# The MLP behind a windowed attention rebuilt: wide units, one activation table, VectorE in GpSimd's place

## The chip, the cores and the metric

One core of one Trainium2 chip runs the whole program. The metric is the device time of one execution in microseconds (us), the median of several. The profile is one execution, recorded by the hardware's own profiler. Engine names: PE is TensorE (PEld its weight loads), ACT is ScalarE, DVE is VectorE, POOL is GpSimd, SP is SyncE, which here only issues DMAs.

## The reference, cut to what matters

Attention over 4 batches x 8 heads x 768 positions x 64 channels, where each position sees the 128 last positions and the first 4 ("sinks"). Its output, 3072 tokens x 512, goes through an MLP whose activation is a rational function of h:

```python
x = attn_out.transpose(0, 2, 1, 3).reshape(B * S, H * D)      # 3072 x 512
h = x @ w_in                                                  # 3072 x 2048
h2 = h * h
h3 = h2 * h
P = a[0] + a[1] * h + a[2] * h2 + a[3] * h3
Q = 1.0 + np.abs(b[0]) * np.abs(h) + np.abs(b[1]) * h2
g = P / (Q + 1e-06)
return (g @ w_out).astype(np.float32)                         # 3072 x 512
```

## The kernel before, in words

The program has two stages. **Attention** loops over the 32 heads. For each head three DMAs bring q, k and v (`q_in` and `v_in` on SP's queue, `k_in` on ACT's); they are cast to bf16, q and k are transposed on PE, and three pairs of 128-row tiles go through scores (`ps_s`), Exp on ACT (`e_t`), the mask product (`a_t`, on DVE for the first pair, on POOL for the other two), the product with v (`ps_o`), a reciprocal on DVE and a scaling (`o_bf`), and a transpose back (`ps_xall`). The last step of a head is the copy of `ps_xall` into the resident bf16 matrix `xT` (L199 before), so 32 of these copies mark the 32 heads. Four `xT` tiles of 128 rows hold the MLP's input, channels on the partitions.

**The MLP** loops over 6 blocks of 512 tokens, and in each over 8 chunks of 2 x 128 of the 2048 hidden channels, so 48 chunks of 128 partitions x 1024 elements. A chunk is eight matmuls into `ps_h` (two PSUM banks of fp32), then eleven elementwise operations on three engines: ACT takes Square and Abs straight from PSUM, DVE makes three linear forms of h*h (`t2`, `t1`, `sden`) and `u_num`, which reads PSUM, POOL adds `p_num` and `den`, ACT takes Ln and Exp(-x) of `den` as the reciprocal, and DVE multiplies to `g_t`:

```python
nc.gpsimd.tensor_tensor(out=p_num, in0=u_num, in1=t1, op=ALU.add)
nc.gpsimd.tensor_tensor(out=den, in0=sden, in1=hb, op=ALU.add)
nc.scalar.activation(out=lnq, in_=den, func=AF.Ln)
nc.scalar.activation(out=rden, in_=lnq, func=AF.Exp, scale=-1.0)
nc.vector.tensor_tensor(out=g_t, in0=p_num, in1=rden, op=ALU.mult)
```

After the eighth chunk of a block, four accumulations of 16 matmuls make `ps_out` (128 tokens x 512), ACT copies each to `o_t`, and SP's queue stores it.

The kernel's text gives no order between engines. A scheduler of the language orders each engine's instructions, and each engine runs its own list strictly in order; pools of `bufs` buffers decide when a tile may be written again. Pools that are closed give their memory to later ones, and the first writer of the later pool then waits for the last reader of the earlier.

At the start, POOL's queue (its DMAs cast fp32 to bf16 as they copy) issues the four loads of `w_in`, the sixteen of `w_out`, then `a_bc` and `b_bc` (the coefficients, broadcast to all partitions), while SP and ACT issue the first q, k, v.

Of the kernel before, what the change touches and what calls it, by code (L numbers as in the profile page):

```python
# [16 lines left out]
def kernel(  # L17
# [25 lines left out]
    const_pool = ctx.enter_context(tc.tile_pool(name="const", bufs=1))
    wpool = ctx.enter_context(tc.tile_pool(name="weights", bufs=1))
    xpool = ctx.enter_context(tc.tile_pool(name="xT", bufs=1))
# [16 lines left out]
        out=mask_prev, in_=ones_pp, pattern=[[-1, P]], compare_op=ALU.is_gt,  # L62
# [25 lines left out]
    a_bc = const_pool.tile([P, 4], FP32)  # L88
# [13 lines left out]
    with tc.tile_pool(name="a_in", bufs=2) as a_in, \  # L102
# [7 lines left out]
        for b in range(B):  # L110
            for h in range(H):
# [19 lines left out]
                for t in range(NT):  # L131
# [7 lines left out]
                                 start=True, stop=True)  # L139
# [64 lines left out]
    a0 = a_bc[:, 0:1]
    a1 = a_bc[:, 1:2]
    a2 = a_bc[:, 2:3]
    a3 = a_bc[:, 3:4]
    b0 = babs[:, 0:1]
    b1 = babs[:, 1:2]

    with tc.tile_pool(name="m_ps", bufs=2, space=bass.MemoryType.PSUM) as m_ps, \
         tc.tile_pool(name="m_sb", bufs=2) as m_sb, \
         tc.tile_pool(name="g_sb", bufs=2) as g_sb_pool, \
         tc.tile_pool(name="o_ps", bufs=2, space=bass.MemoryType.PSUM) as o_ps, \
         tc.tile_pool(name="o_sb", bufs=2) as o_sb:
        TW = 2 * TB
        for blk in range(NB):
            t0 = blk * TB
            g_chunks = []
            for fp in range(NFFC // 2):  # L220
                ps_h = m_ps.tile([P, 2, TB], FP32, tag="ps_h")
# [7 lines left out]
                s_sq = m_sb.tile([P, TW], BF16, tag="s_sq")
                nc.scalar.activation(out=s_sq, in_=ps_h, func=AF.Square)  # L230
                hb = m_sb.tile([P, TW], BF16, tag="hb")
                nc.scalar.activation(out=hb, in_=ps_h, func=AF.Abs, scale=b0)  # L232
                t2 = m_sb.tile([P, TW], BF16, tag="t2")
                nc.vector.tensor_scalar(out=t2, in0=s_sq, scalar1=a3, scalar2=a1,  # L234
                                        op0=ALU.mult, op1=ALU.add)
                t1 = m_sb.tile([P, TW], BF16, tag="t1")
                nc.vector.tensor_scalar(out=t1, in0=s_sq, scalar1=a2, scalar2=a0,  # L237
                                        op0=ALU.mult, op1=ALU.add)
                u_num = m_sb.tile([P, TW], BF16, tag="u_num")
                nc.vector.tensor_tensor(out=u_num, in0=ps_h, in1=t2, op=ALU.mult)  # L240
                p_num = m_sb.tile([P, TW], BF16, tag="p_num")
                nc.gpsimd.tensor_tensor(out=p_num, in0=u_num, in1=t1, op=ALU.add)  # L242
                sden = m_sb.tile([P, TW], BF16, tag="sden")
                nc.vector.tensor_scalar(out=sden, in0=s_sq, scalar1=b1, scalar2=1.000001,
                                        op0=ALU.mult, op1=ALU.add)
                den = m_sb.tile([P, TW], BF16, tag="den")
                nc.gpsimd.tensor_tensor(out=den, in0=sden, in1=hb, op=ALU.add)  # L247
                lnq = m_sb.tile([P, TW], FP32, tag="lnq")
                nc.scalar.activation(out=lnq, in_=den, func=AF.Ln)  # L249
                rden = m_sb.tile([P, TW], BF16, tag="rden")  # L250
                with nc.allow_low_precision(reason="exp(-ln(q)) reciprocal, tol 2e-2"):
                    nc.scalar.activation(out=rden, in_=lnq, func=AF.Exp, scale=-1.0)  # L252
                g_t = g_sb_pool.tile([P, TW], BF16, tag=f"g_{fp}")
                nc.vector.tensor_tensor(out=g_t, in0=p_num, in1=rden, op=ALU.mult)  # L254
                g_chunks.append(g_t)

            for tt in range(TB // P):
                ps_out = o_ps.tile([P, DM], FP32, tag="ps_out")
                for fc in range(NFFC):
                    fp, half = fc // 2, fc % 2  # L260
                    nc.tensor.matmul(ps_out,  # L261
                                     lhsT=g_chunks[fp][:, half * TB + tt * P:
                                                       half * TB + (tt + 1) * P],
                                     rhs=w_out_sb[fc],
                                     start=(fc == 0), stop=(fc == NFFC - 1))
                o_t = o_sb.tile([P, DM], FP32, tag="o_t")
                nc.scalar.activation(out=o_t, in_=ps_out, func=AF.Copy)
                row0 = t0 + tt * P
                nc.sync.dma_start(out=out[row0:row0 + P, :], in_=o_t)


# [33 lines left out]
```

## Time and profile before

| what | us |
|---|---|
| median of 3 runs (630.08 to 630.91) | 630.25 |
| span of the profiled execution, first to last instruction | 628.0 |
| so outside the span, by the median | 2.25 |
| start of the span to the first `xT` copy | 44.2 |
| first to last `xT` copy (31 heads) | 223.2 |
| last `xT` copy to the end of the last `g_t` | 346.2 |
| from there to the end of the span | 14.4 |

The stages are cut where an instruction that belongs to one of them ends it. The busy time of an engine in a stage, beside the stage's length, says whether it can be what sets the pace there; the durations of single instructions say what a changed one would cost.

### The profile page before, as it was taken

How to read it: one execution, taken by the hardware profiler on the slowest of the kernel's cores; microseconds unless marked ns; L12 is line 12 of the kernel's file. 1: busy time of each engine (PE TensorE's matmuls, PEld its weight loads, DVE VectorE, ACT ScalarE, POOL GpSimd, SP SyncE). 2: the span in 40 equal slices, each digit the busy share in tenths (PEclk: the TensorE clock that was granted, in tenths of full speed). 3: DMA queues.
4: the chain of work that ended last, by engine and by line, in shares of the span. 5: the costliest groups of instructions: out<-in, count | busy, mean ns of one | idle time of the engine just before them, and what ended most of it. 6: DMA issues, size and time to landing. Idle time of an engine off the chain costs nothing.

```text
span 628.0 us, 6817 instructions
## 1 busy us (share of the span) xinstructions
PE 448.3 (71%) x2208; PEld 209.6 (33%) x2208; DVE 353.8 (56%) x666; ACT 459.4 (73%) x602; POOL 309.9 (49%) x255
## 2 busy tenths in 40 slices
PE   2289998888888889946569566755846595567626
PEld 2145555555555555311123122211311231223102
DVE  1134444444444444397774976687397739766860
ACT  1265565555555555279999899999999999999891
POOL 4514433333334433256654664575467537645750
PEclk9999999999999999987779768977897787789667
DMA  9982233333333321000001000000100010000001
GB/s 191 203 162 53 63 76 82 84 75 77 77 77 86 78 64 39 1 0 1 1 0 67 2 0 34 34 0 1 50 18 0 0 67 1 0 33 35 0 0 67
DMA packets 81699, 29.80 MB, mean 47 GB/s; under 512 B 76032, under 2 KB 78080, under 8 KB 81664
## 3 DMA queue, kind: packets, MB, share of 16 engines
q1 hardware_dynamic: 53632, 18.88, 12.1%
q10 hardware_dynamic: 25088, 6.29, 4.5%
q0 software_dynamic: 2944, 4.20, 3.6%
q8 instruction: 17, 0.28, 0.2%
q14 instruction: 18, 0.15, 0.1%
HBM read 27.27 MB, written 6.29 MB: 53 GB/s over the span
## 4 chain that ended last, share of the span: by engine, by line
PE 30%; ACT 29%; DVE 16%; issue 14%; POOL 6%; DMA 5%; POOLq 0%; ACTq 0%; DVEq 0%
ACT L252 7%; ACT rden L252 6%; ACT lnq L249 5%; ACT L249 5%; PE ps_s L161 5%; PE ps_xall L196 5%; PE ps_tk L133 4%; DMA q_in<-in_q_dram 4%; DVE t L234 4%; PE ps_o L176 4%; PE ps_o L183 3%; POOL den L247 3%; PE ps_tq L132 3%; PE ps_sink L138 3%; DVE g_t L254 3%
## 5 line engine op out<-in xcount | busy, mean ns | idle before, releaser
L225 PE MATMUL ps_h<-xT,w_in_sb 128*128 128x512 bf16 x384 | 124.9, 474 | 65.1 <-DVE u_num L240 63.9
L247 POOL TENSOR_TENSOR den<-sden,hb 128x1024 bf16<-128x1024 bf16 x48 | 104.4, 2176 | 132.8 <-ACT hb L232 92.7
L261 PE MATMUL ps_out<-w_out_sb,g_t 128*128 128x512 bf16 x384 | 114.6, 452 | 65.9 <-DVE g_t L254 65.8
L171 POOL TENSOR_TENSOR a_t<-e_t,mask_pp 128x512 bf16<-128x512 bf16 x64 | 73.6, 1150 | 142.6 <-PE ps_o L179 117.3
L254 DVE TENSOR_TENSOR g_t<-p_num,rden 128x1024 bf16<-128x1024 bf16 x48 | 88.2, 1838 | 75.1 <-ACT rden L252 75.1
L242 POOL TENSOR_TENSOR p_num<-u_num,t 128x1024 bf16<-128x1024 bf16 x48 | 104.4, 2174 | 9.3 <-DVE u_num L240 9.3
L164 ACT ACTIVATE e_t<-ps_s 128x512 bf16<-128x512 f32 (+1 forms) x96 | 53.0, 554 | 54.0 <-POOL a_t L171 51.8
L225 PEld LDWEIGHTS <-w_in_sb 128*128 128x128 bf16 x384 | 43.9, 115 | 135.9 <-issue 108.5
L261 PEld LDWEIGHTS <-g_t 128*128 128x128 bf16 x384 | 39.1, 110 | 140.6 <-DVE g_t L254 91.0
L187 DVE RECIPROCAL recip<-ps_o 128x1 f32<-128x1 f32 x192 | 29.4, 164 | 99.6 <-PE ps_o L183 94.9
L190 ACT ACTIVATE o_bf<-ps_o,recip 128x64 bf16<-128x64 f32 x96 | 29.5, 307 | 54.6 <-DVE recip L187 52.0
L240 DVE TENSOR_TENSOR u_num<-ps_h,t 128x1024 bf16<-128x1024 f32 x48 | 58.6, 1220 | 16.8 <-ACT hb L232 16.8
L161 PE MATMUL ps_s<-qT,kT 64*128 64x128 bf16 x352 | 53.6, 301 | 13.8 <-ACT e_t L164 13.8
L249 ACT ACT_TABLE_LOAD x48 | 61.6, 1283 | 0.9
L252 ACT ACT_TABLE_LOAD x48 | 61.6, 1283 | 0.8
L249 ACT ACTIVATE lnq<-den 128x1024 f32<-128x1024 bf16 x48 | 50.8, 1058 | 15.2 <-POOL den L247 14.8
L232 ACT ACTIVATE hb<-ps_h,babs 128x1024 bf16<-128x1024 f32 x48 | 53.0, 1104 | 0.0
L252 ACT ACTIVATE rden<-lnq 128x1024 bf16<-128x1024 f32 x48 | 50.7, 1057 | 0.5
L230 ACT ACTIVATE s_sq<-ps_h 128x1024 bf16<-128x1024 f32 x48 | 48.5, 1011 | 1.7 <-PE ps_xall L196 1.7
L234 DVE TENSOR_SCALAR t<-s_sq,a_bc 128x1024 bf16<-128x1024 bf16 x48 | 47.5, 990 | 3.8 <-ACT s_sq L230 3.8
L196 PE MATMUL ps_xall<-ident,o_bf 128*64 128x128 bf16 x192 | 44.8, 311 | 3.0 <-ACT o_bf L190 2.0
L237 DVE TENSOR_SCALAR t<-s_sq,a_bc 128x1024 bf16<-128x1024 bf16 x48 | 45.6, 950 | 0.0
(51 smaller groups left out, 557.3 us busy)
## 6 DMA issues: line engine op xcount, KB each, us to landing
k_in<-in_k_dram ACTq DMA_DIRECT2D x32, 192.0 KB, 3.0
q_in<-in_q_dram SPq DMA_DIRECT2D x32, 192.0 KB, 2.7
v_in<-in_v_dram SPq DMA_DIRECT2D x32, 192.0 KB, 2.7
out_dram<-o_t SPq DMA_DIRECT2D x24, 256.0 KB, 2.0
w_in_sb<-in_moe_w_in_dram POOLq DMA_DIRECT2D x4, 512.0 KB, 10.9
w_out_sb<-in_moe_w_out_dram POOLq DMA_DIRECT2D x16, 128.0 KB, 7.5
a_bc<-in_moe_a_dram POOLq DMA_DIRECT2D x1, 2.0 KB, 6.4
b_bc<-in_moe_b_dram POOLq DMA_DIRECT2D x1, 1.0 KB, 5.8
```

What stands on the lines that cost most here:

```text
L161: nc.tensor.matmul(ps_s[:, co:co + P], lhsT=kT[:, kt * P:(kt + 1) * P], rhs=qT[:, t * P:(t + 1) * P], start=True, stop=True)
L171: nc.gpsimd.tensor_tensor(out=a_t[:, 0:ncols], in0=e_t[:, 0:ncols], in1=pmask, op=ALU.mult)
L196: nc.tensor.transpose(ps_xall[:, t * P:(t + 1) * P], o_bf, ident)
L225: nc.tensor.matmul(ps_h[:, half, :], lhsT=w_in_sb[c][:, fc * P:(fc + 1) * P], rhs=xT[c][:, t0:t0 + TB], start=(c == 0), stop=(c == NDMC - 1))
L234: nc.vector.tensor_scalar(out=t2, in0=s_sq, scalar1=a3, scalar2=a1, op0=ALU.mult, op1=ALU.add)
L240: nc.vector.tensor_tensor(out=u_num, in0=ps_h, in1=t2, op=ALU.mult)
L242: nc.gpsimd.tensor_tensor(out=p_num, in0=u_num, in1=t1, op=ALU.add)
L247: nc.gpsimd.tensor_tensor(out=den, in0=sden, in1=hb, op=ALU.add)
L249: nc.scalar.activation(out=lnq, in_=den, func=AF.Ln)
L252: nc.scalar.activation(out=rden, in_=lnq, func=AF.Exp, scale=-1.0)
L254: nc.vector.tensor_tensor(out=g_t, in0=p_num, in1=rden, op=ALU.mult)
L261: nc.tensor.matmul(ps_out, lhsT=g_chunks[fp][:, half * TB + tt * P: half * TB + (tt + 1) * P], rhs=w_out_sb[fc], start=(fc == 0), stop=(fc ...
```

## The change

The attention code is the same; the lists that the scheduler makes of it are not. The MLP's code is new:

- A unit is 4 x 128 hidden channels x 512 tokens, 128 x 2048 elements, so 24 units in place of 48 chunks.
- ACT copies `ps_h` from PSUM to a bf16 tile `hb` (two copies of 1024 for a unit), and all that follows reads `hb`.
- |h| is an AND of the pairs of bf16 numbers, taken as 32-bit words, with a mask that clears the two sign bits (`den`, 128 x 1024 words on DVE). h*h is a product on DVE, in every fourth unit a Square on ACT. The sum |h| + h*h, the odd and the even part of the numerator and their sum are DVE's; GpSimd has nothing left in the MLP.
- h is scaled by |b1|/|b0|, which is multiplied into `w_in` once. So `w_in` is no longer cast by its DMA: SP loads it as fp32 into two staging buffers (`t_f`, 1 MB each), and DVE scales and casts it. That needs `b_bc`, through `babs` (ACT) and a few tiny DVE operations to `csc`.
- Ln takes scale and bias as per-partition operands; one activation table, loaded at the start, holds all functions that are used.
- The units are pipelined by hand: unit i's projection, then Ln and Exp of unit i-1, then numerator and denominator of unit i, then one output tile of an earlier block, then `g_t` of unit i-1.

```diff
+    nc.scalar.preload_act_table_set("natural_log_exp_and_others")
...
-    w_in_sb = []
-    for c in range(NDMC):
-        t_in = wpool.tile([P, DF], BF16, name=f"w_in_sb_{c}")
-        nc.gpsimd.dma_start(out=t_in, in_=moe_w_in[c * P:(c + 1) * P, :])
-        w_in_sb.append(t_in)
...
+    csc = const_pool.tile([P, 1], FP32)
+    nc.vector.tensor_tensor(out=csc, in0=bpos[:, 1:2], in1=binv[:, 0:1], op=ALU.mult)
...
+    with tc.tile_pool(name="w_stage", bufs=2) as w_stage:
+        for c in range(NDMC):
+            t_f = w_stage.tile([P, DF], FP32, tag="w_in_f")
+            nc.sync.dma_start(out=t_f, in_=moe_w_in[c * P:(c + 1) * P, :])
+            t_in = wpool.tile([P, DF], BF16, name=f"w_in_sb_{c}")
+            nc.vector.tensor_scalar(out=t_in, in0=t_f, scalar1=csc, scalar2=None,
+                                    op0=ALU.mult)
+            w_in_sb.append(t_in)
...
+                nc.scalar.activation(out=hb[:, half * 2 * TB:(half + 1) * 2 * TB],
+                                     in_=ps_h, func=AF.Copy)
+            return hb
+
+        def numerator_and_denominator(i, hb):
+            s_sq = m_sb.tile([P, UW], BF16, tag="s_sq")
+            den = m_sb.tile([P, UW], BF16, tag="den")
+            if i % 4 == 3:
+                nc.scalar.activation(out=s_sq, in_=hb, func=AF.Square)
+            else:
+                nc.vector.tensor_tensor(out=s_sq, in0=hb, in1=hb, op=ALU.mult)
+            nc.vector.tensor_scalar(out=den.bitcast(U32), in0=hb.bitcast(U32),
+                                    scalar1=0x7FFF7FFF, scalar2=None,
+                                    op0=ALU.bitwise_and)
+            nc.vector.tensor_tensor(out=den, in0=den, in1=s_sq, op=ALU.add)
+            odd = m_sb.tile([P, UW], BF16, tag="odd")
+            nc.vector.tensor_scalar(out=odd, in0=s_sq, scalar1=a3, scalar2=a1,
+                                    op0=ALU.mult, op1=ALU.add)
+            num = m_sb.tile([P, UW], BF16, tag="num")
+            nc.vector.tensor_scalar(out=num, in0=s_sq, scalar1=a2, scalar2=a0,
+                                    op0=ALU.mult, op1=ALU.add)
+            nc.vector.tensor_tensor(out=odd, in0=odd, in1=hb, op=ALU.mult)
+            nc.vector.tensor_tensor(out=num, in0=num, in1=odd, op=ALU.add)
+            return den, num
+
+        def reciprocal(den):
+            lnq = m_sb.tile([P, UW], FP32, tag="lnq")
+            nc.scalar.activation(out=lnq, in_=den, func=AF.Ln, scale=qsc, bias=one_eps)
+            rden = m_sb.tile([P, UW], BF16, tag="rden")
+            with nc.allow_low_precision(reason="exp(-ln(q)) reciprocal, tol 2e-2"):
+                nc.scalar.activation(out=rden, in_=lnq, func=AF.Exp, scale=-1.0)
+            return rden
...
+        for i in range(len(units) + 1):
+            hb = project_in(i) if i < len(units) else None
+            rden = reciprocal(pend[1]) if pend is not None else None
+            nxt = None
+            if hb is not None:
+                den, num = numerator_and_denominator(i, hb)
+                nxt = (i, den, num)
+            if waiting:
+                project_out(*waiting.pop(0))
+            if pend is not None:
+                blk, u = units[pend[0]]
+                g_t = g_sb_pool.tile([P, UW], BF16, tag=f"g_{u}")
+                nc.vector.tensor_tensor(out=g_t, in0=pend[2], in1=rden, op=ALU.mult)
+                g_of[blk, u] = g_t
+                if u == NU - 1:
+                    waiting += [(blk, tt) for tt in range(ntt)]
+            pend = nxt
```

Two places of the built lists. The first is the head of ACT's list, at the start of the program. Before:

```order
L116 DMA k_in<-in_k_dram 128x6x64 x2
L121 ACT_TABLE_LOAD
L121 ACTIVATE q_bf<-q_in 128x384
L116 DMA k_in<-in_k_dram 128x6x64
L121 ACTIVATE q_bf<-q_in 128x384
```

The same place after the change (L143 is the load of k, L148 the cast of q, L90 the absolute value of the coefficients b):

```order
L44 ACT_TABLE_LOAD
L90 ACTIVATE babs<-b_bc 128x2
L143 DMA k_in<-in_k_dram 128x6x64 x2
L148 ACTIVATE q_bf<-q_in 128x384
L143 DMA k_in<-in_k_dram 128x6x64 x2
L161 ACTIVATE qT<-ps_tq 64x768
```

`babs`, which waits for the last DMA of POOL's queue, now stands ahead of the first load of k. In the same way SP's list now begins with the four loads of `t_f`, and the first q, k and v, whose buffers lie where the staging buffers were, wait for the fourth scaling of `w_in` on DVE.

The second place is DVE's list in the middle of the MLP. Before, one chunk (`t` is t2 and t1):

```order
L234 TENSOR_SCALAR t_4360<-s_sq,a_bc 128x1024
L237 TENSOR_SCALAR t_4362<-s_sq,a_bc 128x1024
L244 TENSOR_SCALAR sden<-s_sq,babs 128x1024
L240 TENSOR_TENSOR u_num<-ps_h,t_4360 128x1024
L254 TENSOR_TENSOR g_t<-p_num,rden 128x1024
```

After, one unit (`acoef` holds the rescaled coefficients a):

```order
L272 TENSOR_TENSOR s_sq<-hb 128x2048
L273 TENSOR_SCALAR den<-hb 128x1024
L278 TENSOR_SCALAR odd<-s_sq,acoef 128x2048
L276 TENSOR_TENSOR den<-den,s_sq 128x2048
L281 TENSOR_SCALAR num<-s_sq,acoef 128x2048
L283 TENSOR_TENSOR odd<-odd,hb 128x2048
L321 TENSOR_TENSOR g_t<-num,rden 128x2048
L284 TENSOR_TENSOR num<-num,odd 128x2048
```

Two chunks of five operations became one unit of eight, in every fourth unit seven (the first row is then ACT's). `g_t` in the seventh row belongs to the unit before, and stands behind three operations of the next unit that do not wait for ACT's Ln and Exp.

## Rows read from the trace of the kernel before

**Rows 1.** Busy time of each engine in four stages (clock granted, DMA share, GB/s behind).

```profile
core 0: us, PE busy (x) PEld busy (x) DVE busy (x) ACT busy (x) POOL busy (x), PEclk, DMA share, GB/s
0.00:44.20 44.20, 18.58 (x128) 12.33 (x128) 8.43 (x34) 15.51 (x31) 19.21 (x41) 1.00 1.04 193
44.20:267.40 223.20, 203.46 (x1331) 115.90 (x1331) 94.96 (x391) 114.29 (x261) 83.85 (x119) 1.00 0.29 66
267.40:613.60 346.20, 215.75 (x716) 77.31 (x716) 250.43 (x241) 327.20 (x308) 206.83 (x96) 0.80 0.04 16
613.60:628.00 14.40, 10.49 (x36) 4.04 (x36) 0.00 (x0) 2.39 (x4) 0.00 (x0) 0.82 0.20 73
```

**Rows 2.** Single lines on ACT in the MLP: ns min/median/max, first and last start.

```profile
L230 ACT ACTIVATE s_sq<-ps_h x48: 1002/1006/1034, 267.5 to 601.3; 128x1024 bf16<-128x1024 f32 x48
...
L232 ACT ACTIVATE hb<-ps_h,babs x48: 1092/1097/1135, 268.5 to 604.6; 128x1024 bf16<-128x1024 f32 x48
...
L252 ACT ACT_TABLE_LOAD  x48: 1283/1283/1283, 273.9 to 610.4; - x48
L252 ACT ACTIVATE rden<-lnq x48: 1056/1057/1057, 275.2 to 611.7; 128x1024 bf16<-128x1024 f32 x48
...
L267 ACT ACTIVATE o_t<-ps_out x24: 577/592/598, 328.6 to 624.2; 128x512 f32<-128x512 f32 x24
```

**Rows 3.** Single lines on DVE, the same columns.

```profile
L254 DVE TENSOR_TENSOR g_t<-p_num,rden x48: 677/2400/2605, 276.4 to 612.9; 128x1024 bf16<-128x1024 bf16 x48
...
L168 DVE TENSOR_TENSOR a_t<-e_t,mask_p x32: 329/337/358, 26.9 to 254.3; 128x384 bf16<-128x384 bf16 x32
...
L234 DVE TENSOR_SCALAR t<-s_sq,a_bc x48: 533/537/2336, 268.6 to 603.8; 128x1024 bf16<-128x1024 bf16 x48
...
L122 DVE CAST k_bf<-k_in x32: 340/352/721, 4.8 to 242.9; 128x384 bf16<-128x384 f32 x32
...
L240 DVE TENSOR_TENSOR u_num<-ps_h,t x48: 1209/1224/1226, 269.9 to 605.7; 128x1024 bf16<-128x1024 f32 x48
```

**Rows 4.** Timeline of the MLP from 383 to 391 us: start, duration, engine, line, operation.

```profile
383.02 2.11 POOL L242 TENSOR_TENSOR p_num<-u_num,t 128x1024 bf16<-128x1024 bf16 x1
...
383.29 2.40 DVE L254 TENSOR_TENSOR g_t<-p_num,rden 128x1024 bf16<-128x1024 bf16 x1 [1.22 <-ACT rden L252]
...
385.61 0.53 DVE L234 TENSOR_SCALAR t<-s_sq,a_bc 128x1024 bf16<-128x1024 bf16 x1
...
386.07 0.53 DVE L237 TENSOR_SCALAR t<-s_sq,a_bc 128x1024 bf16<-128x1024 bf16 x1
...
389.94 0.69 DVE L254 TENSOR_TENSOR g_t<-p_num,rden 128x1024 bf16<-128x1024 bf16 x1 [2.94 <-ACT rden L252]
...
390.97 2.12 POOL L247 TENSOR_TENSOR den<-sden,hb 128x1024 bf16<-128x1024 bf16 x1 [5.84 <-ACT hb L232]
```

**Rows 5.** The same timeline, weight loads of PE, one for each 512-column matmul.

```profile
387.37 0.15 PEld L261 LDWEIGHTS <-g_t 128*128 128x128 bf16 x1 [0.28 <-issue]
...
387.80 0.15 PEld L261 LDWEIGHTS <-g_t 128*128 128x128 bf16 x1 [0.28 <-issue]
...
395.43 2.25 PEld L225 LDWEIGHTS <-w_in_sb 128*128 128x128 bf16 x11
```

**Rows 6.** Timeline of the first 45 us.

```profile
4.27 0.52 ACT L121 ACTIVATE q_bf<-q_in 128x384 bf16<-128x384 f32 x1 [0.98 <-DMA q_in<-in_q_dram]
...
27.78 0.54 POOL L91 DMA_DIRECT2D b_bc<-in_moe_b_dram  x1 [0.29 <-DMA w_out_sb<-in_moe_w_out_dram]
```

**Rows 7.** DMA view of the first 40 us: a queue's packets, MB written, share of 16 engines; issues.

```profile
q0 software_dynamic: 2944, 4.20, 57.2%
...
k_in<-in_k_dram ACTq DMA_DIRECT2D x9, 192.0 KB, 4.7
```

**Rows 8.** The copies that end a head.

```profile
L199 DVE COPY xT<-ps_xall x32: 548/550/552, 44.2 to 267.4; 64x768 bf16<-64x768 bf16 x32
```

More of the change, by code (lines that the diff above doesn't have):

```diff
@@ L11 @@
 BF16 = mybir.dt.bfloat16
+U32 = mybir.dt.uint32
 AF = mybir.ActivationFunctionType
@@ L93 @@
     nc.scalar.activation(out=babs, in_=b_bc, func=AF.Abs)
+    bpos = const_pool.tile([P, 2], FP32)
+    nc.vector.tensor_scalar(out=bpos, in0=babs, scalar1=1e-9, scalar2=None, op0=ALU.max)
+    binv = const_pool.tile([P, 2], FP32)
+    nc.vector.reciprocal(out=binv, in_=bpos)
+    csc = const_pool.tile([P, 1], FP32)
+    nc.vector.tensor_tensor(out=csc, in0=bpos[:, 1:2], in1=binv[:, 0:1], op=ALU.mult)
+    cinv = const_pool.tile([P, 1], FP32)
+    nc.vector.tensor_tensor(out=cinv, in0=bpos[:, 0:1], in1=binv[:, 1:2], op=ALU.mult)
+    qsc = const_pool.tile([P, 1], FP32)
+    nc.vector.tensor_tensor(out=qsc, in0=bpos[:, 0:1], in1=cinv, op=ALU.mult)
+    acoef = const_pool.tile([P, 4], FP32)
+    nc.vector.tensor_copy(out=acoef[:, 0:1], in_=a_bc[:, 0:1])
+    cpow = const_pool.tile([P, 3], FP32)
+    nc.vector.tensor_copy(out=cpow[:, 0:1], in_=cinv)
+    nc.vector.tensor_tensor(out=cpow[:, 1:2], in0=cinv, in1=cinv, op=ALU.mult)
+    nc.vector.tensor_tensor(out=cpow[:, 2:3], in0=cpow[:, 1:2], in1=cinv, op=ALU.mult)
+    nc.vector.tensor_tensor(out=acoef[:, 1:4], in0=a_bc[:, 1:4], in1=cpow, op=ALU.mult)
+    one_eps = const_pool.tile([P, 1], FP32)
+    nc.vector.memset(one_eps, 1.000001)
+    w_in_sb = []
+    with tc.tile_pool(name="w_stage", bufs=2) as w_stage:
[6 more added lines that the diff above has]
+            w_in_sb.append(t_in)
     xT = []
@@ L203 @@
     NB = NTOK // TB
[L204 to L209, printed above, removed]
+    NU = 4
+    UC = NFFC // NU
+    UW = UC * TB
+    a0 = acoef[:, 0:1]
+    a1 = acoef[:, 1:2]
+    a2 = acoef[:, 2:3]
+    a3 = acoef[:, 3:4]
+    units = [(blk, u) for blk in range(NB) for u in range(NU)]
+    ntt = TB // P
     with tc.tile_pool(name="m_ps", bufs=2, space=bass.MemoryType.PSUM) as m_ps, \
@@ L214, with project_in @@
          tc.tile_pool(name="o_ps", bufs=2, space=bass.MemoryType.PSUM) as o_ps, \
-         tc.tile_pool(name="o_sb", bufs=2) as o_sb:
-        TW = 2 * TB
-        for blk in range(NB):
+         tc.tile_pool(name="o_sb", bufs=3) as o_sb:
+        g_of = {}
+        def project_in(i):
+            blk, u = units[i]
             t0 = blk * TB
-            g_chunks = []
-            for fp in range(NFFC // 2):
+            hb = m_sb.tile([P, UW], BF16, tag="hb")
+            for half in range(UC // 2):
                 ps_h = m_ps.tile([P, 2, TB], FP32, tag="ps_h")
-                for half in range(2):
-                    fc = 2 * fp + half
+                for j in range(2):
+                    fc = u * UC + half * 2 + j
                     for c in range(NDMC):
-                        nc.tensor.matmul(ps_h[:, half, :],
+                        nc.tensor.matmul(ps_h[:, j, :],
                                          lhsT=w_in_sb[c][:, fc * P:(fc + 1) * P],
@@ L228 @@
                                          start=(c == 0), stop=(c == NDMC - 1))
[L229 to L269, printed above, removed]
+                nc.scalar.activation(out=hb[:, half * 2 * TB:(half + 1) * 2 * TB],
+                                     in_=ps_h, func=AF.Copy)
@@ new lines, in reciprocal, with project_out @@
+        def reciprocal(den):
[5 more added lines that the diff above has]
+            return rden
+        def project_out(blk, tt):
+            ps_out = o_ps.tile([P, DM], FP32, tag="ps_out")
+            for fc in range(NFFC):
+                g_t = g_of[blk, fc // UC]
+                co = (fc % UC) * TB + tt * P
+                nc.tensor.matmul(ps_out, lhsT=g_t[:, co:co + P], rhs=w_out_sb[fc],
+                                 start=(fc == 0), stop=(fc == NFFC - 1))
+            o_t = o_sb.tile([P, DM], FP32, tag="o_t")
+            nc.scalar.activation(out=o_t, in_=ps_out, func=AF.Copy)
+            row0 = blk * TB + tt * P
+            nc.sync.dma_start(out=out[row0:row0 + P, :], in_=o_t)
@@ new lines @@
+        waiting = []
+        pend = None
+        for i in range(len(units) + 1):
[15 more added lines that the diff above has]
+            pend = nxt
@@ L273 @@
+        for w in waiting:
+            project_out(*w)
 _INS = ['q', 'k', 'v', 'n_sink', 'window', 'moe_w_in', 'moe_w_out', 'moe_a', 'moe_b']
```

## The prediction, made before the changed kernel ran

> **What bounds the kernel now.** I read the busy times by stage first [rows 1]. To 44.2 us the DMA engines are full (share 1.04) and the first heads starve. From there to 267.4 the remaining 31 heads take 7.2 us each; no engine is at its limit by busy time except PE (203 of 223 us), and PE's lists are chained by waits for the other engines. From 267.4 to 613.6 ACT is busy 327.2 of 346.2 us: ACT sets the pace of the MLP, at 346.2/48 = 7.2 us a chunk, 14.4 us for what will be one unit. DVE (250) and PE (216) have room, and the granted clock of PE is 0.80.
>
> The single lines say what ACT does in a chunk [rows 2]: Square 1.006, Abs 1.097, Ln and Exp 1.057 each, two table loads of 1.283 each (48 at Ln, 48 at Exp), and half an `o_t` of 0.592: 7.1 us. The loads are 2.57 of it.
>
> DVE's lines need their minimum, not only their mean [rows 3]: `g_t`, 128x1024, takes between 0.677 and 2.605 us. The timeline shows why [rows 4]: at 383.29 it takes 2.40 while POOL runs `p_num`; at 389.94 it takes 0.69, and POOL does nothing until 390.97. L234 has the same spread (0.533 to 2.336). I read the short ones as DVE's own price and the long ones as POOL's doing; the rival below takes them the other way.
>
> **The change part by part.** It is a new MLP stage, so I price the stage afresh by engine, and then the start and the attention.
>
> *DVE, a unit.* A product of two bf16 tiles: 0.329 at 384 elements and 0.677 at 1024 without POOL [rows 3], so 0.544 ns an element, and 0.677 + 0.557 = 1.23 us at 2048. Back to back an instruction starts 0.07 before the last one's end (385.61 + 0.53 against 386.07) [rows 4], so 1.16. There are five (h*h, `den`, `odd`, `num`, `g_t`): 5.82. A linear form with two scalars took 0.533 at 1024; it reads one tensor, and no row has another width. Between no growth (0.533) and doubling (1.07) I take half the product's growth: 0.81, so 0.74 in sequence, two of them 1.48. The AND on 1024 words of 32 bits has no row. Below stands the cast from 32-bit input, 0.352 at 384 against 0.337 for the bf16 product of that size, so 0.69 at 1024; above `u_num`, one element at a time from PSUM, 1.224 [rows 3]. I take 0.69, 0.62 in sequence: the cast is the nearer row, SBUF to SBUF with 32-bit words. Sum: 5.82 + 1.48 + 0.62 = 7.92 us, and 6.76 where ACT takes the square. 18 x 7.92 + 6 x 6.76 = 183 us. Bounds: the AND at its upper row +13 us, the linear forms at theirs +13 or -13 us.
>
> *ACT, a unit.* Two copies from PSUM at 1.006; Exp 1.057 + 1024 x 0.81 ns (from `o_t` and Square: 0.592 at 512, 1.006 at 1024) = 1.89; Ln the same plus two per-partition operands at 0.09 (1.097 against 1.006) = 2.07; `o_t` 0.59; a quarter of a Square, 0.47 [rows 2]. 7.0 us, under DVE's 7.6 on average. Table loads: none, 123 us off ACT. Is ACT's answer late? From the end of `den` to the end of Exp stand Ln, one copy and Exp: 5.0 us, 5.6 with an `o_t`. DVE has, by its list, the rest of this unit, `g_t` of the unit before and six operations of the next to do before it needs that Exp: 9.8 us. So ACT waits for DVE, and the wait is hidden while ACT stays under about 9 us.
>
> *PE, a unit.* 16 matmuls in and 16 out. At full clock eleven weight loads take 2.25 us, so 0.215 apart; at the lower level (1.2 of 2.4 GHz) they are 0.43 apart [rows 5]. 6.9 us or 13.8. At full clock PE is under DVE by 0.7 us a unit; that is all the cover it has.
>
> *POOL.* Its 96 additions, some 2.1 us each, go from the MLP [rows 4]; their work is in DVE's sum.
>
> *Ends of the MLP.* DVE starts the first unit about half a microsecond after the last `xT` copy, as ACT did before (267.5 after 267.4) [rows 2, 8]. After the last unit's sum one `g_t` is left, 1.2 us, and then what took 14.4 us with 36 matmuls [rows 1]; now 40 are left (8 of two open tiles, 32 of two whole ones), 15.4.
>
> *The start.* This part loses. Before, the first q was cast at 4.27 us, and `b_bc` was issued at 27.78 [rows 6] and delayed nobody. Now ACT's first k, SP's first q and v and POOL's first cast stand behind `b_bc`, the scalings and four `t_f`. The casting queue wrote 4.20 MB in 0.572 x 40 = 22.9 us of all sixteen DMA engines [rows 7]; `w_out` is half of that, 11.4 us. A `t_f` of 1.05 MB at the same rate of written bytes (183 GB/s) is 5.7 us; two of them may start at once. All this is through at about 3 + 11.4 + 11.5 = 26 us, and `b_bc` is last. `babs` and the tiny operations to `csc`: 1 us (each under the 0.33 of a 384-element product [rows 3]). The first scaling, 0.35 + 1664 x 0.544 ns = 1.26, ends at 28.3 and frees the buffer for the third `t_f`; two more take 11.5, to 40; the last scaling ends at 41. Then q, k and v come in up to 4.7 us [rows 7]: the first q at 45, 41 us later than before. But the old start ran through full DMA queues to its first `xT` at 44.2. The new one finds them empty: I give the first head 15 us, two head times, since each head passes three dependent pairs while the next is prepared. First `xT` at 60, 16 us late. Bounds: 50 (`w_out` and `t_f` faster, one head time) and 75 (`b_bc` as late as before, then the same steps).
>
> *The attention.* Same instructions, another list: bounded by the 7.2 us a head [rows 8] and its own chain, I leave 223.2 us, with ten either way.
>
> Sum: 60 + 223.2 + 0.5 + 183.1 + 1.2 + 15.4 = 483.4 us of span against 628.0. The profiled execution lies 2.25 under the median of the runs, so 485.7: **486 us**, 23% faster. 0.2% is about what a measurement of this kernel can tell from no change; it plays no part here.
>
> **The rivals.**
>
> *PE becomes the bound because its clock falls.* Before, the clock was 0.80 over the MLP with PE busy 216 of 346 us [rows 1]. At 0.80 a unit is 6.9/0.80 = 8.6 us, 206 in all, 23 more than DVE: 509. At the lower level throughout, 13.8 x 24 = 331: 634, no better than before. For it: the first block's units have no output matmuls, so PE works 16 x 0.215 = 3.4 us of each unit and pauses, and later ones wait for `g_t` in strict order. Against: with output matmuls PE has 6.9 of 7.6 us to do, and in attention, busy at 203 of 223 us, the clock was 1.00 [rows 1]. The Trainium skill, TensorE: Matmul & The Clock Gate, section on psum-queue depth-cycling, warns that short idle spells of PE between matmul groups throttle it again and again; by that rule this rival happens, and the time is its 509. The trace has it in the old MLP, with longer gaps, and the trace alone decides its chance.
>
> *The products on DVE keep their long times.* If 2.4 us at 1024 elements were the product's own nature and not POOL's, 4.75 products a unit would take 4.75 x 2.4 x 1.8 = 20.5 us, with the rest 22.6, and the units 543: 846 us, far slower than before. It turns where the units take 328 us, 13.65 each: a product of 2.43 us at 2048, twice my price. Against it stands each `g_t` of 0.69 with POOL idle, beside 2.40 with POOL at work [rows 4]. The Trainium skill, GPSIMD Engine Reference, section Specifications, says that GpSimd's SBUF interfaces are shared with VectorE and that VectorE instructions with two SBUF inputs, or in a two-port mode, contend for them. By that rule this rival falls, the units cost 183 us and not 543, and the trace agrees with it in these two rows.
>
> *The AND runs at one element at a time*, 1.22 us: 499 us. For it: no row shows a bit operation. Against: the cast.
>
> *The start or the attention's list costs more*, a first `xT` at 75 or 7.5 us a head: 495 to 510.
>
> *The better side*: linear forms that hardly grow, and a first `xT` at 50: 463 to 475.
>
> **How the numbers follow.** Forecast, DVE-bound with the start 10 to 22 us late: 0.52, its own range 475 to 496. PE-bound by its clock 0.14, of it 0.01 at the lower level throughout. AND slow 0.12. Start or attention dearer 0.10. Better side 0.10. Products long 0.02. The range 462 to 516 leaves out the ends of the better side, of the dear start and of PE's rival, under 2 in 10. Faster 0.97, the same 0.01, slower 0.02.
>
> **What would show it.** DVE busy over 90% of the MLP, with products of 128x2048 at 1.2 us and little spread; the AND at 0.7; ACT waiting for `den`, never DVE for `rden`; one table load in all; PE at 0.9 of the clock or more once output matmuls run. The first q cast at some 45 us and the first `xT` near 60; 31 heads in 213 to 233 us. I am wrong if DVE idles in the MLP for PE's or ACT's sake, if products spread although POOL rests, or if the start takes over 75 us.

## The result and the profile after

The changed kernel takes 487.03 us (median of 4 runs, 486.38 to 487.50) against 630.58 for the kernel before in the same comparison: 0.771 of its time, 95% interval 0.769 to 0.774. Forecast were 486. The profiled execution has a span of 485.3 us.

The first reading is the table by stage, cut as in [rows 1] at the first and the last `xT` copy and at the end of the last `g_t`; the columns are those of [rows 1].

```profile
0.00:50.30 50.30, 13.13 (x94) 9.08 (x94) 13.40 (x46) 10.02 (x20) 16.19 (x37) 1.00 0.80 181
50.30:287.80 237.50, 204.56 (x1360) 121.38 (x1360) 107.77 (x394) 125.11 (x272) 86.16 (x119) 1.00 0.30 69
287.80:470.10 182.30, 163.35 (x715) 70.03 (x715) 179.33 (x187) 158.16 (x122) 0.00 (x0) 0.97 0.08 29
470.10:485.30 15.20, 11.24 (x43) 4.58 (x43) 0.00 (x1) 2.39 (x4) 0.00 (x0) 0.84 0.19 69
```

| stage | before | forecast | after |
|---|---|---|---|
| start to the first `xT` copy | 44.2 | 60 | 50.3 |
| 31 heads | 223.2 | 223.2 | 237.5 |
| MLP to the end of the last `g_t` | 346.2 | 184.8 | 182.3 |
| from there to the end | 14.4 | 15.4 | 15.2 |
| outside the span | 2.25 | 2.25 | 1.7 |

The MLP gives 164 us. The stages ahead of it lose 20, which the forecast had as 16, but in the wrong place: the start was 10 us better and the heads 14 us worse than predicted; their 237.5 us lie outside the 213 to 233 that the prediction named. That the total is right to a microsecond is therefore partly luck.

In the MLP, DVE is busy 179.3 of 182.3 us. Its single lines answer to [rows 3] (ns, minimum, median, maximum):

```profile
L272 DVE TENSOR_TENSOR s_sq<-hb x18: 1204/1213/1224, 291.2 to 454.4; 128x2048 bf16<-128x2048 bf16 x18
...
L273 DVE TENSOR_SCALAR den<-hb x24: 674/680/686, 292.3 to 462.1; 128x1024 uint32<-128x1024 uint32 x24
...
L278 DVE TENSOR_SCALAR odd<-s_sq,acoef x24: 796/803/808, 292.9 to 462.7; 128x2048 bf16<-128x2048 bf16 x24
...
L321 DVE TENSOR_TENSOR g_t<-num,rden x24: 1205/1211/1226, 303.2 to 468.9; 128x2048 bf16<-128x2048 bf16 x24
```

The spread is gone: a product is 1.205 to 1.226 us every time, where `g_t` at half the width ran from 0.677 to 2.605 before. The timeline of DVE shows the same back to back, as [rows 4] did with gaps (start, duration):

```profile
390.69 0.81 DVE L281 TENSOR_SCALAR num<-s_sq,acoef 128x2048 bf16<-128x2048 bf16 x1
391.41 1.21 DVE L283 TENSOR_TENSOR odd<-odd,hb 128x2048 bf16<-128x2048 bf16 x1
392.55 1.21 DVE L321 TENSOR_TENSOR g_t<-num,rden 128x2048 bf16<-128x2048 bf16 x1
393.68 1.21 DVE L284 TENSOR_TENSOR num<-num,odd 128x2048 bf16<-128x2048 bf16 x1
```

ACT's lines answer to [rows 2]; the table load is there once, at 0.8 us:

```profile
L262 ACT ACTIVATE hb<-ps_h x48: 999/1010/1035, 287.9 to 455.0; 128x1024 bf16<-128x1024 f32 x48
...
L289 ACT ACTIVATE lnq<-den,one_eps,qsc x24: 2088/2096/2102, 294.9 to 464.6; 128x2048 f32<-128x2048 bf16 x24
...
L292 ACT ACTIVATE rden<-lnq x24: 1897/1900/1924, 297.8 to 466.8; 128x2048 bf16<-128x2048 f32 x24
...
L44 ACT ACT_TABLE_LOAD  x1: 1283/1283/1283, 0.8 to 0.8; - x1
```

The view of waits for the MLP (total us, times, longest; two of its rows) has ACT and PE waiting for DVE, and no row in which DVE waits for `rden`:

```profile
ACT lnq L289 <- DVE den L276: 19.7, 17, 2.0
PE ps_out L300 <- DVE g_t L321: 13.5, 8, 4.0
```

The start answers to [rows 6] (timeline). `babs` ran 4 us after `b_bc` was issued, the third and the fourth scaling waited for their `t_f`, and the first q was cast 3.5 us after the fourth scaling freed the memory.

```profile
14.90 0.54 POOL L88 DMA_DIRECT2D b_bc<-in_moe_b_dram  x1 [0.17 <-issue]
18.89 0.20 ACT L90 ACTIVATE babs<-b_bc 128x2 f32<-128x2 f32 x1 [16.80 <-DMA b_bc<-in_moe_b_dram]
19.72 1.29 DVE L118 TENSOR_SCALAR w_in_sb<-t_f,csc 128x2048 bf16<-128x2048 f32 x1
25.86 1.29 DVE L118 TENSOR_SCALAR w_in_sb<-t_f,csc 128x2048 bf16<-128x2048 f32 x1 [3.19 <-DMA t_f<-in_moe_w_in_dram]
29.02 1.29 DVE L118 TENSOR_SCALAR w_in_sb<-t_f,csc 128x2048 bf16<-128x2048 f32 x1 [1.87 <-DMA t_f<-in_moe_w_in_dram]
33.85 0.52 ACT L148 ACTIVATE q_bf<-q_in 128x384 bf16<-128x384 f32 x1 [14.75 <-DMA q_in<-in_q_dram]
```

The DMA view of the first 20 us answers to [rows 7]:

```profile
q0 software_dynamic: 2368, 2.10, 64.6%
q1 hardware_dynamic: 288, 2.10, 26.7%
```

Both queues wrote 2.10 MB. The casting queue (`w_out`) took 0.646 x 20 = 12.9 us of all sixteen engines, the plain one (two `t_f`) 0.267 x 20 = 5.3 us. The forecast had priced the plain loads at the casting queue's rate. These are sums of packet times, and packets overlap: from 8 to 17 us, with the casting queue alone, the share is 1.24, and by elapsed time that queue moved 202 GB/s. This cast, fp32 to bf16, reads two bytes for each that it writes, so 202 written are some 404 read (worked out, not measured), near the plain queue's 400. Whether the bytes read set the rate, no run tells.

### The profile page after: what moved, and what is told of

The parts are those of the page before. It is cut to its first block, busy times and chain, and to the rows that moved or that the text cites. A ratio compares the mean times of both kernels' runs of the same rounds, so it can differ in the third digit from the quotient of the medians.

```text
span 485.3 us, 6228 instructions
## 1 busy us (share of the span) xinstructions
PE 392.3 (81%) x2208; PEld 205.1 (42%) x2208; DVE 300.5 (62%) x627; ACT 295.7 (61%) x416; POOL 102.3 (21%) x155
## 4 chain that ended last, share of the span: by engine, by line
PE 44%; DVE 40%; DMA 6%; issue 5%; ACT 3%; POOL 1%; DVEq 0%; ACTq 0%; POOLq 0%
PE ps_s L188 8%; PE ps_xall L223 7%; DVE g_t L321 5%; DVE odd L283 5%; DVE num L284 5%; PE ps_tk L160 5%; PE ps_o L203 5%; PE ps_tq L159 5%; PE ps_o L210 4%; PE ps_out L300 4%; DVE s_sq L272 4%; DVE num L281 4%; PE ps_sink L165 3%; DVE odd L278 3%; DVE den L273 3%
## 5 line engine op out<-in xcount | busy, mean ns | idle before, releaser
L258 PE MATMUL ps_h<-xT,w_in_sb 128*128 128x512 bf16 x384 | 93.8, 392 | 3.0 <-ACT hb L262 3.0
L160 PE MATMUL ps_tk<-ident,k_bf 128*64 128x128 bf16 x192 | 37.5, 313 | 47.3 <-DVE k_bf L149 45.6
L289 ACT ACTIVATE lnq<-den,one_eps,qsc 128x2048 f32<-128x2048 bf16 x24 | 50.3, 2096 | 19.8 <-DVE den L276 19.7
L262 ACT ACTIVATE hb<-ps_h 128x1024 bf16<-128x1024 f32 x48 | 48.6, 1012 | 6.0 <-PE ps_xall L223 3.3
L203 PE MATMUL ps_o<-v_ext,a_t 128*128 128x65 bf16 x192 | 40.3, 237 | 8.8 <-DVE a_t L195 8.5
L292 ACT ACTIVATE rden<-lnq 128x2048 bf16<-128x2048 f32 x24 | 45.7, 1903 | 0.0
L223 PEld LDWEIGHTS <-o_bf 128*64 128x64 bf16 x192 | 24.8, 143 | 37.4 <-ACT o_bf L217 13.9
L206 PE MATMUL ps_o<-v_ext,a_t 128*128 128x65 bf16 x160 | 39.2, 245 | 0.0
L151 POOL CAST v_ext<-v_in 128x384 bf16<-128x384 f32 x32 | 16.2, 506 | 100.2 <-PE ps_o L210 67.7
L188 PEld LDWEIGHTS <-kT 64*128 64x128 bf16 x352 | 31.3, 130 | 11.8 <-issue 8.2
L159 PE MATMUL ps_tq<-ident,q_bf 128*64 128x128 bf16 x192 | 33.9, 314 | 0.0
L161 ACT ACTIVATE qT<-ps_tq 64x768 bf16<-64x768 bf16 x32 | 25.5, 797 | 13.3 <-PE ps_tq L159 10.6
```

The lines of the kernel that those rows point to most:

```text
L159: nc.tensor.transpose(ps_tq[:, t * P:(t + 1) * P], q_bf[:, t, :], ident)
L160: nc.tensor.transpose(ps_tk[:, t * P:(t + 1) * P], k_bf[:, t, :], ident)
L223: nc.tensor.transpose(ps_xall[:, t * P:(t + 1) * P], o_bf, ident)
L258: nc.tensor.matmul(ps_h[:, j, :], lhsT=w_in_sb[c][:, fc * P:(fc + 1) * P], rhs=xT[c][:, t0:t0 + TB], start=(c == 0), stop=(c == NDMC - 1))
L262: nc.scalar.activation(out=hb[:, half * 2 * TB:(half + 1) * 2 * TB], in_=ps_h, func=AF.Copy)
L289: nc.scalar.activation(out=lnq, in_=den, func=AF.Ln, scale=qsc, bias=one_eps)
```

## The experiments

Each kernel was timed beside the kernel before. "After" is the changed kernel, 487.03 us.

**k1_cast: `w_in` cast by its DMA again, h scaled by ACT's copy instead.**

```diff
+        nc.gpsimd.dma_start(out=t_in, in_=moe_w_in[c * P:(c + 1) * P, :])
...
-            t_f = w_stage.tile([P, DF], FP32, tag="w_in_f")
...
-                                     in_=ps_h, func=AF.Copy)
+                                     in_=ps_h, func=AF.Copy, scale=csc)
```

Expected: 

> The changed kernel with w_in loaded and cast by its DMA ahead of w_out, as before, and the factor |b1|/|b0| applied as a per-partition scale in ACT's copies of h instead. The lists of the attention are then those of the kernel before. My theory: the 20 us that the changed kernel reaches the MLP later (last xT copy at 287.8 against 267.4) are the staging's doing, 6 by the late start (50.3 against 44.2) and 14 by the list that the scheduler makes behind it (237.5 against 223.2 us for 31 heads). Then the last xT copy stands at 267.4, the MLP behind it takes its 197.5, as ACT's copies may grow by 0.09 while ACT waits for DVE: 467 us, 464 to 470. Rival 1: only the late start comes back, and the heads' slower pace has another cause in the new kernel: 481. Rival 2: the longer copies are on the path: 48 x 0.09 = 4 us more, 471.

Measured: 469.05 us, ratio 0.742 (0.7385 to 0.7454). The `xT` copies run from 45.5 to 268.5, so the start is 5 us and the heads are 14.5 us shorter than after (18.0 in all by the medians). The theory's 464 to 470 holds, and the longer copies are not on the path: the MLP took 181.3 us, against 182.3 after. The staging of `w_in`, as it stands in after, costs the whole of that, and most of it long after the staging has ended; k9 below shows that staging as such need not.

**k2_pool: the last addition of the numerator on GpSimd.**

```diff
-            nc.vector.tensor_tensor(out=num, in0=num, in1=odd, op=ALU.add)
+            nc.gpsimd.tensor_tensor(out=num, in0=num, in1=odd, op=ALU.add)
```

Expected: 

> The changed kernel with one of DVE's additions, num + odd, given back to GpSimd. Theory: while GpSimd works on two tiles, DVE's two-tensor and two-port instructions stand still, so the unit pays GpSimd's time, 2 x 2.12 = 4.2 us for 2048, in place of DVE's 1.16: 7.6 - 1.2 + 4.2 = 10.6 us a unit, 73 more in all, 560 us, and products beside it last up to 5 us. Rival: the two work side by side and DVE is relieved of 1.16 us a unit, to ACT's 7.0: 473 us. Between: if DVE only slows by half, 510.

Measured: 551.16 us, ratio 0.873 (0.870 to 0.876), 64 us slower than after although DVE has 24 additions fewer. The timeline of k2 shows one addition on POOL and what DVE did beside it, with two one-tensor operations of the same execution:

```profile
427.90 4.92 POOL L284 TENSOR_TENSOR num<-num,odd 128x2048 bf16<-128x2048 bf16 x1 [3.69 <-DVE odd L283]
```

```profile
420.22 4.54 DVE L278 TENSOR_SCALAR odd<-s_sq,acoef 128x2048 bf16<-128x2048 bf16 x1
...
427.68 1.21 DVE L321 TENSOR_TENSOR g_t<-num,rden 128x2048 bf16<-128x2048 bf16 x1
428.97 4.93 DVE L272 TENSOR_TENSOR s_sq<-hb 128x2048 bf16<-128x2048 bf16 x1
433.82 0.68 DVE L273 TENSOR_SCALAR den<-hb 128x1024 uint32<-128x1024 uint32 x1
...
439.43 4.40 DVE L273 TENSOR_SCALAR den<-hb 128x1024 uint32<-128x1024 uint32 x1
```

The DVE operation that begins while POOL's runs (428.97) ends 1.08 us after POOL's end (432.82), about its own length: it waited POOL out. POOL's addition in turn began at 427.90, while DVE's `g_t` ran to 428.89; it took 4.92 us where the shortest of the 24 took 4.06, the 0.9 more being about the rest of `g_t`. In this execution DVE's wait also befell one-tensor operations, a linear form of 4.54 us and an AND of 4.40. The MLP took 246.9 us, 10.3 a unit, about DVE's 7.6 less a product of 1.14, plus some 4 of POOL's. The Trainium skill, GPSIMD Engine Reference, section Specifications, names this contention for DVE operations with two SBUF inputs or in a two-port mode; the run agrees for the two-input ones and gives the size, the whole rest of POOL's operation; whether the one-tensor ones run in such a mode, no run here shows.

**k3_nopreload: without the line that loads one table.** The compiler then puts a load at every Ln and every Exp.

```diff
-    nc.scalar.preload_act_table_set("natural_log_exp_and_others")
```

Expected: 

> The changed kernel without the one table set: two table loads a unit, 48 in all, since Ln and Exp come from different sets again. Theory: ACT has 7.0 of DVE's 7.57 us to do, so 2 x 1.283 = 2.57 us more make ACT the bound at 9.6 us a unit: 24 x 2.0 = 48 more, 535 us. Rival: the loads hide in ACT's waits for DVE: 487. The Trainium skill, ScalarE: Activation LUTs, section What ACT_TABLE_LOAD costs, counts some 2.66 us for a switch of sets; by that ACT would need 12.3 us a unit and the time be 600.

Measured: 533.13 us, ratio 0.844 (0.840 to 0.847). ACT is the bound: it is busy 222.4 of the MLP's 228.2 us, and DVE waits 42.1 us for `rden`. In ACT's timeline each operation follows the load by 0.01 to 0.02 us:

```profile
402.83 1.28 ACT L291 ACT_TABLE_LOAD   x1
404.12 1.91 ACT L291 ACTIVATE rden<-lnq 128x2048 bf16<-128x2048 f32 x1
405.94 1.00 ACT L261 ACTIVATE hb<-ps_h 128x1024 bf16<-128x1024 f32 x1
406.96 1.28 ACT L288 ACT_TABLE_LOAD   x1
```

So a switch costs 1.28 us, and some 1.4 with the gaps beside it and the 0.09 by which two operations overlap where no load stands between them (404.12 + 1.91 against 405.94). The Trainium skill, ScalarE: Activation LUTs, section What ACT_TABLE_LOAD costs, gives the same 1283 ns and adds a drain of about 1380 ns; no such time stands in this trace, and the run decides for the load alone.

**k4_before_tables: the kernel before with that line, and nothing else.**

```diff
+    nc.scalar.preload_act_table_set("natural_log_exp_and_others")
```

Expected: 

> The kernel before with the one table set and nothing else of the change: 96 table loads of 1.283 us go. Rival, the simple sum: ACT was the bound, so all 123 us come off: 507 us. My theory: DVE's two-port instructions and GpSimd's additions take turns, so a chunk needs GpSimd's 2 x 2.12 and DVE's 0.53 + 0.53 + 0.47 + 0.69 one after the other, about 6.2 us, 300 in all, and little of the 123 is left to gain: 565 to 595 us, with DVE's products long and ACT idle for a third of the MLP.

Measured: 587.01 us, ratio 0.931 (0.926 to 0.935). Of 123 us of loads 44 come back. ACT now waits for `den` from POOL (91.2 us), and DVE's lines say why (busy us, mean ns; idle before):

```profile
L235 DVE TENSOR_SCALAR t<-s_sq,a_bc 128x1024 bf16<-128x1024 bf16 x48 | 92.8, 1933 | 6.9 <-ACT s_sq L231 6.9
L255 DVE TENSOR_TENSOR g_t<-p_num,rden 128x1024 bf16<-128x1024 bf16 x48 | 71.1, 1482 | 20.7 <-ACT rden L253 18.7 <-POOL p_num L243 2.0
```

A linear form that takes 0.533 alone [rows 3] has a mean of 1.933: it and POOL take turns. The theory's 565 to 595 holds. With GpSimd out of the MLP the same line is worth 46 us of 61.6 us of loads (k3), where it gave 44 of 123 here.

**k7_dvesq: all squares on DVE.**

```diff
-            if i % 4 == 3:
+            if False:
```

Expected: 

> The changed kernel with all 24 squares on VectorE, none on ScalarE. Theory: VectorE sets the pace of the MLP, so six products of 1.213 us, 1.14 to 1.16 in sequence, are added to the path: plus 6.9 us, 494 us, and ScalarE's idle time grows by six Squares of 1.915 and these 6.9. Rival: TensorE (6.9 us a unit, and waits for g_t) or ScalarE sets it, with VectorE's fullness only apparent: 487.

Measured: 493.18 us, 6.2 more than after, ratio 0.781 (0.779 to 0.783). The MLP (last `xT` to the end of `g_t`) took 188.5 us, 6.2 more, so about 1.03 for each of six products. DVE sets the pace; neither PE nor ACT hid the added work.

**k5_1024: units of half the width.**

```diff
-    NU = 4
+    NU = 8
```

Expected: 

> The changed kernel with units of 1024 columns, 48 of them, all else the same. Theory: what the width saves is the part of an instruction's time that does not grow with it. VectorE then has five products of 0.677 (0.607 in sequence), two linear forms of 0.533 (0.463), one AND of some 0.40 (0.33): 4.29 us a unit, 3.68 without the square, 36 x 4.29 + 12 x 3.68 = 199 us for the MLP against 182: 502 us. Rival A: width is worth nothing, because VectorE's time goes with columns: 487. Rival B: with units half as long the pipeline's cover for Ln and Exp no longer does and VectorE waits for rden: over 515.

Measured: 502.67 us, ratio 0.796 (0.795 to 0.798), as the sum of the lines said. The lines of k5:

```profile
L272 DVE TENSOR_TENSOR s_sq<-hb x36: 682/687/698, 289.6 to 478.3; 128x1024 bf16<-128x1024 bf16 x36
...
L273 DVE TENSOR_SCALAR den<-hb x48: 418/423/432, 290.2 to 482.6; 128x512 uint32<-128x512 uint32 x48
...
L278 DVE TENSOR_SCALAR odd<-s_sq,acoef x48: 540/544/553, 290.5 to 482.9; 128x1024 bf16<-128x1024 bf16 x48
```

Two halves cost 1.374, 0.846 and 1.088 where the whole took 1.213, 0.680 and 0.803. The width itself is worth 15.6 us of the 143.6.

**k6_serial: no pipelining by hand;** each unit is written whole, and a block's output tiles behind its last unit.

```diff
-        for i in range(len(units) + 1):
...
+        for i in range(len(units)):
+            hb = project_in(i)
+            den, num = numerator_and_denominator(i, hb)
+            rden = reciprocal(den)
...
+            if u == NU - 1:
+                for tt in range(ntt):
+                    project_out(blk, tt)
```

Expected: 

> The changed kernel without the hand-written pipeline: each unit is written whole, projection, numerator and denominator, Ln and Exp, g_t, and after a block's last unit its four output tiles; the scheduler may still interleave. Theory: by its list g_t of a unit stands 4 to 5 us of VectorE work behind that unit's den sum, sometimes 3.1, and Ln, a copy and Exp take 5.0 us (5.6 with an o_t): VectorE waits some 1 us a unit, plus 24, and the output matmuls come in blocks of 64, during which ps_h is late once a block, plus 0 to 10: 505 to 520 us. Rival: the scheduler's interleaving does as well as the hand-written order: 487. Third case: the waits add up to a full Ln and Exp a unit (4 us): 580.

Measured: 490.76 us, ratio 0.779 (0.776 to 0.781). The theory falls. The MLP is 5.6 us longer than after (187.9), not 20 to 30, and of it DVE waits 4.7 us for `rden`, in five places. The scheduler interleaves the units itself; I had read its list against a Ln, a copy and an Exp, 5.0 us, but waits of that kind stand at five of 24 units only. What follows the last `g_t` is 2.5 us shorter than after (12.7 against 15.2), so in the medians the hand-written order is worth 3.7 us.

**k9_stage: after, with the pool of the staging buffers left open,** so that q, k and v do not lie in its memory.

```diff
-    with tc.tile_pool(name="w_stage", bufs=2) as w_stage:
+    w_stage = ctx.enter_context(tc.tile_pool(name="w_stage", bufs=2))
```

Expected: 

> The changed kernel, but the pool of the two staging buffers t_f stays open to the end, so that no later pool is given its memory; all else is the same, w_in is still staged as fp32 and scaled on VectorE. Theory: the head loads stand behind the staging only because q_in, k_in and v_in lie in the memory of t_f and so wait for the last scaling; with memory of their own the first q, k and v come early again (the list now has ACT's first k ahead of babs), the first xT copy is at 45 to 48 as in the kernel before (44.2), not 50.3, and the heads' list, which the scheduler builds from another start, is again at about 7.2 us a head: 469 to 475 us. Rival A: the volume of the staging (4 MB of fp32 more on the queues and four scalings on DVE among the first heads) is what costs: 483 to 490. Rival B: the start comes back but the list of heads stays at 7.66 us a head: 481 to 483.

Measured: 437.76 us, ratio 0.694 (0.692 to 0.696), far under the theory and both rivals. The start came back, and by more than I thought (first `xT` at 41.7, not 45 to 48). The heads did not return to the old pace, they beat it: 199.3 us for 31. The windows below are five heads of after, six of k9 and five of k1, each in its repeating part (columns as in [rows 1]):

```profile
106.41:145.12 38.71, 33.01 (x228) 20.20 (x227) 17.83 (x66) 20.84 (x45) 14.30 (x20) 1.00 0.34 77
```

```profile
109.00:146.00 37.00, 36.92 (x272) 24.86 (x272) 20.03 (x80) 22.74 (x54) 16.47 (x24) 1.00 0.43 97
```

```profile
100.70:138.20 37.50, 33.47 (x228) 19.47 (x227) 15.74 (x66) 19.79 (x46) 14.06 (x21) 1.00 0.35 80
```

PE stands idle 5.7 us in the first, 0.1 in the second, 4.0 in the third. The copies of `xT` show the patterns: after repeats every five heads, 38.6 us (117.47 to 156.07), with one gap of 11;

```profile
117.47 0.55 DVE L226 COPY xT<-ps_xall 64x768 bf16<-64x768 bf16 x1 [1.18 <-PE ps_xall L223]
...
145.12 0.55 DVE L226 COPY xT<-ps_xall 64x768 bf16<-64x768 bf16 x1
156.07 0.55 DVE L226 COPY xT<-ps_xall 64x768 bf16<-64x768 bf16 x1 [1.18 <-PE ps_xall L223]
```

k9 takes 12.29 for two heads;

```profile
134.40 0.54 DVE L227 COPY xT<-ps_xall 64x768 bf16<-64x768 bf16 x1
140.65 0.55 DVE L227 COPY xT<-ps_xall 64x768 bf16<-64x768 bf16 x1
146.69 0.54 DVE L227 COPY xT<-ps_xall 64x768 bf16<-64x768 bf16 x1
```

and k1, like the kernel before, 7.50 for one.

```profile
130.68 0.55 DVE L221 COPY xT<-ps_xall 64x768 bf16<-64x768 bf16 x1 [0.65 <-PE ps_xall L218]
138.18 0.55 DVE L221 COPY xT<-ps_xall 64x768 bf16<-64x768 bf16 x1 [0.65 <-PE ps_xall L218]
```

**k10_four: k9 with four staging buffers.** This tells list from memory: memory as in k9, list of the heads as in k1.

```diff
-    w_stage = ctx.enter_context(tc.tile_pool(name="w_stage", bufs=2))
+    w_stage = ctx.enter_context(tc.tile_pool(name="w_stage", bufs=4))
```

Expected: 

> The kernel k9 (staging pool kept open) with four staging buffers in place of two, nothing else. Its loads of t_f all stand ahead of the first q, and the scheduler's list for VectorE is, from the seventh head to the end, word for word that of k1 and of the kernel before (7.50 us a head there), not that of k9 (6.15 us a head in its steady part). Theory: the list alone sets the heads' pace; the memory only decides when the first head may start. Then the first xT copy is at 42 to 46, the heads' cadence is 7.50, 31 heads take 220 to 226 us, and with 198 us behind the last xT the time is 461 to 470 us. Rival: k9's gain of 24 us in the heads comes from the memory that is not shared, or from w_in not being cast by its DMA: 438 to 445.

Measured: 474.00 us, ratio 0.752 (0.750 to 0.753). The timeline of k10:

```profile
49.31 0.55 DVE L227 COPY xT<-ps_xall 64x768 bf16<-64x768 bf16 x1
...
93.04 0.55 DVE L227 COPY xT<-ps_xall 64x768 bf16<-64x768 bf16 x1 [0.65 <-PE ps_xall L224]
100.53 0.55 DVE L227 COPY xT<-ps_xall 64x768 bf16<-64x768 bf16 x1 [0.65 <-PE ps_xall L224]
```

The pace is 7.50 again, 227.0 us for 31 heads: the rival falls, the list sets the pace. In the traces TensorE, VectorE, ScalarE and GpSimd each run their operations in the same order in k10, in k1 and in the kernel before (eight heads, from 100.5 to 160.6 us in k10); in k9 and in after the order of each is another. The time missed its 461 to 470, by the start above all: the first `xT` stands at 49.3, not 42 to 46, since with four `t_f` ahead of it in SP's queue the first q is issued at 19.85 us.

**k11_third and k9_again: k9 with the square on ACT in every third unit, and k9 beside it.**

```diff
-            if i % 4 == 3:
+            if i % 3 == 2:
```

Expected of k11: 

> The kernel k9 (staging pool kept open) with the square on ScalarE in every third unit, not every fourth: eight, not six. Theory: VectorE sets the pace of the MLP, so two products of 1.16 us in sequence fall from the path: 2.3 us under k9 in the same comparison, about 435.5 us; ScalarE's 7.2 us a unit stays under VectorE's 7.5. Rival: ScalarE's Square delays the copy hb or the Ln behind it, so that VectorE waits for what it saves: the same as k9 or 1 to 3 us more.

Expected of k9 again: 

> The kernel k9 once more, as the measure for the other two in the same comparison: 436 to 440 us.

Measured: 435.25 us, ratio 0.689 (0.688 to 0.690), beside 437.73 for k9. The MLP took 178.8 us against 181.1, the 2.3 that two products are worth. It is the fastest of all the kernels: 0.894 of the changed kernel's time, by the medians.

## Why the prediction was right, and where not

**The bound of the MLP: right, and shown.** DVE is busy 98% of the stage, k7 lengthens it by 6.2 us for six products more, k11 shortens it by 2.3 for two fewer. The prices were 1.23, 0.81 and 0.69 us; 1.212, 0.803 and 0.680 were measured. In sequence a product took 1.135 (391.41 to 392.55 to 393.68 in the timeline above), not 1.16, and the units took 178.9 us (291.2 to 470.1), not 183.1. Two edges were off the other way and by an error of counting: the first `s_sq` starts 3.4 us after the last `xT` copy, not 0.5, since it waits for `hb`; and the 1.2 for a last `g_t` was already in the units' sum. 3.4 + 178.9 is the 182.3 of the table. The other two engines were priced well too: ACT's 7.0 us a unit were 6.6 (158.2 of the stage), PE's 6.9 were 6.8.

**Short products once GpSimd rests: right, and shown by k2.** The rival of long products falls.

**ACT's loads: right.** One load is left. k3 shows what they would still cost here (46 us), k4 what their removal alone gives (44).

**The clock: right.** The granted clock was 0.97 over the MLP with PE busy 163 of 182 us; the rival at 509 us did not happen. The old 0.80 went with PE busy 216 of 346 us [rows 1].

**The AND: right,** 0.680 against 0.69; the rival at 499 falls.

**The start: the step that failed is "at the same rate of written bytes (183 GB/s)".** Plain loads go at 2.10 MB in 5.3 us of the engines, 400 GB/s, so a `t_f` costs 2.7 us of them, not 5.7. With that the same chain gives 3 + 11.4 + 5.3 = 19.7 for `b_bc`, where the forecast had 26 and `babs` ran at 18.9: 7 us of the error. The third and fourth `t_f`, 11.5 us in the forecast and 5.3 at this rate, took 8.0, from the end of the first scaling at 21.0 to the start of the last at 29.0: 3.5 us more of it. The 15 us for the first head after its q were 16.5, which took 1.5 back.

**The attention: the step that failed is "Same instructions, another list ... I leave 223.2 us, with ten either way".** The list decided by far more than ten: the same instructions took 237.5, 223.0 and 199.3 us in after, k1 and k9. In after, POOL waits 67.7 us for `ps_o` at `v_ext`, with mask products behind it in its list, and PE waits for `k_bf` and `a_t`. In k9 POOL has that wait at `v_ext` once, for 0.7 us, and in k1 and k10 never; that it is the cause was not tried by itself.

The view of waits for the heads of after:

```profile
POOL v_ext L151 <- PE ps_o L210: 67.7, 19, 5.0
POOL a_t L198 <- ACT e_t L191: 55.0, 40, 3.0
```

**Open:** why the scheduler settles in one pattern or another. The runs show that small things at the start (a buffer more, a load in another place) decide it, and k10 that the pace goes with the list. k9's list with shared memory was not run.

## What to carry to other kernels

Where GpSimd and VectorE share a stage, price an operation by its shortest instance and ask what POOL did beside the long ones; in k2 the shared unit cost about the sum of both, not the longer. A gain in one engine comes back only in part where another wait stands close behind it (k4: 44 of 123 us). And where a scheduler orders the engines, a change at the start is a change everywhere: compare the cadence of the repeating part, not only the stage that was edited, and ask of every pool that holds early loads whether its memory goes to the loads behind it. Memory of its own gave k9 8.6 us at the start; the other 38 came from the list that the scheduler then made, which no theory here foresaw: k10 has such memory too, and not that list, and takes 474.00 us.

## What was unexpected in the hardware

VectorE's one-tensor operations, too, were held up by GpSimd (a linear form of 0.80 us took 4.54, an AND of 0.68 took 4.40 in k2), and GpSimd's own addition of 128x2048 took 4.06 to 6.71 us. By their packet times a plain load moved its written bytes at some 400 GB/s and the casting queue at 163 (202 by elapsed time, alone); in bytes read the two are close to each other.
